# Three small instructions of the first five pairs move from VectorE to GpSimd, and the first block of x is loaded before the fifth pair's reciprocals

## The chip, the cores and the metric

The kernel runs on one core of a Trainium2 chip. The metric is the device time of one execution in microseconds (us); the time before is the median of three runs, 1360.91 us (1358.39 to 1362.42). The engines are named as in the profile: PE is TensorE (PEld its weight loads), DVE is VectorE, ACT is ScalarE, POOL is GpSimd, and SP is the engine from whose queue the DMAs are issued.

## The reference

Attention with a threshold, then a two-layer MLP with a parametric ReLU, all in float32:

```python
scores = scale * q @ k^T                       # 8 batches, 8 heads, 576 x 576, head_dim 64
scores = where(scores >= max - tau, scores, -1e9)
attn = exp(scores - max)
attn = attn / (sum(attn) + 1e-9)
x = (attn @ v), heads side by side             # 4608 tokens x 512
h = x @ w_in                                   # 512 -> 2048
out = (max(h, 0) + alpha * min(h, 0)) @ w_out  # 2048 -> 512
```

## The kernel before

Heads are worked in 32 pairs (four pairs of a batch). A pair has nine units of 128 query rows, and one unit is one cycle of the main loop `for i in range(-3, total + TAIL)`; unit u of pair p belongs to cycle 9p + u. A cycle does the mask of its own unit (DVE), the scores of the unit two cycles on (PE), row maxima (DVE) and exponentials (ACT), and the transposes of the masked exponentials (PE). Float32 products are made of high and low parts, so most operands are split in two, by ACT, DVE and POOL.

The other work is written out by hand in a table of cycles: `at_cycle(n, step)` puts a step into the list of cycle n, and when the loop comes to that cycle it issues the list in the order in which it was filled (all pairs first, then the decoding of weights). On PE, ACT, DVE and POOL the instructions run in exactly the order of issue. The order of SP's queue of DMAs is chosen at build time from when each DMA is taken to be ready, so it can differ from the order in the text.

The first five pairs (`WHOLE = 5`) are "whole": their products with v use unsplit operands. During cycles 0 to 48 the kernel also decodes the first 14 pieces of weights, each through a row of steps: five on ACT and DVE, then `rest` (four half-tile operations on POOL) and, one cycle later, `join` (two half-tile operations on POOL).

The division by the row sums is a tail of its own. With o = 9p, a whole pair's tail stands in the cycles o + `FINW`: `recip` (o+9) takes the nine column sums `sm` that the masks have accumulated, makes (sm + 1e-9) times min(sm + 1e-9, 1), and takes the reciprocal; `rturn` (o+10) transposes it on PE into a PSUM tile `rp`, one of four of the pool `ps_m`; `rout` (o+11) copies that out with ACT, stores it to DRAM (`rvd`) and loads it twice as a broadcast (`rb`); `fin_mul` (o+16) multiplies x by it on POOL; `fin_out` (o+17) stores x to DRAM (`xs`). Later pairs have their own table, `FINS`, and no minimum.

The MLP takes tokens in groups of 256. Cycle 49 makes the first two groups ready. `Mlp.step_l1` then loads the first group's x (`load_x`, cycle 49) and splits it into high and low parts on POOL (`split_part`, a copy and a subtraction for each of four chunks: two chunks in cycle 49 + `XO0`, two in the next), and from cycle 49 + `XO0` + 2 on one block of the first layer is issued in each cycle with room for it. A planner (`Mlp.cycle`) adds up the estimated PE time of each cycle for that; cycles with attention-times-v products of the split pairs take no such block. Cycles 4, 49 and 52 have three extra products (`filler`) on PE. After the last cycle `behind` does the rest of the MLP, which keeps PE busy alone.

Of the kernel before, what the change touches and what calls it, by code (L numbers as in the profile page):

```python
# [10 lines left out]
F32 = mybir.dt.float32  # L11
# [5 lines left out]
ALU = mybir.AluOpType  # L17
# [4 lines left out]
P = 128  # L22
# [24 lines left out]
AVW = (5, 7, 9, 11)  # L47
AVS = (5, 6, 10, 11)
FINW = (9, 10, 11, 14, 16, 17, 18)
FINS = (9, 11, 12, 12, 15, 16, 16)  # L50
ACTO, SPLO, PUTO = 1, 2, 1
TH1, TH2, TH3 = 0.75, -0.45, 0.1
XO, XO0 = 1, 2
L2O, L2O0 = 3, 1
P1 = 2
LD = 7
# [1 line left out]
WHOLE = 5  # L58
# [22 lines left out]
def tile_masked_attention_moe(  # L81
# [11 lines left out]
    nc = tc.nc  # L93
# [173 lines left out]
    ap1 = at.enter_context(tc.tile_pool(name="ap1", bufs=1))  # L267
# [35 lines left out]
    class Pair:  # L303
# [329 lines left out]

        def recip(self):
            self.rv = ap1.tile([P, 9], F32, tag="rv", name=f"rv{self.pi}", bufs=2)
            nc.vector.tensor_scalar(self.rv, self.sm, 1e-9, None, op0=ALU.add)
            if self.whole:
                nc.vector.scalar_tensor_tensor(self.rv, self.rv, 1.0, self.rv, op0=ALU.min, op1=ALU.mult)
            nc.vector.reciprocal(self.rv, self.rv)

        def rturn(self):
# [55 lines left out]
    def at_cycle(i, fn, *a):  # L697
        later.setdefault(i, []).append((fn, a))
# [5 lines left out]
    for p in pairs:  # L704
        o = 9 * p.pi
        n = o - 9
        if p.pi > 1:
            at_cycle(n + PREP["lk"], p.load, "k")
            at_cycle(n + PREP["lq"], p.load, "q")
        if p.pi == 1:  # L710
            n += P1
        if p.pi > 0:
            at_cycle(n + PREP["kh"], p.prep_kh)
            at_cycle(n + PREP["kl"], p.prep_kl)
            at_cycle(n + PREP["qh"], p.prep_qh)
            at_cycle(n + PREP["qs"], p.prep_qs)
            at_cycle(n + PREP["ql"], p.prep_ql)
            at_cycle(n + PREP["mk"], p.move_k)
            at_cycle(n + PREP["mk2"], p.move_k2)
            at_cycle(n + PREP["mq"], p.move_q)  # L720
            at_cycle(n + PREP["mq2"], p.move_q2)
            at_cycle(n + PREP["lv"], p.load, "v")
            at_cycle(n + PREP["vh"], p.prep_vh)
            at_cycle(n + PREP["vl"], p.prep_vl)
        fin = FINW if p.whole else FINS
        if p.whole:
            for c, step, j in zip(AVW, (0, 0, 1, 1), (0, 1, 1, 0)):
                at_cycle(o + c, p.avmul, step, j, range(3))
                at_cycle(o + c + 1, p.avmul, step, j, range(3, 5))
                at_cycle(o + c + 2, p.avout, step, j)  # L730
        else:
            for c, step, j in zip(AVS, (0, 0, 1, 1), (0, 1, 1, 0)):
                at_cycle(o + c, p.avmul, step, j)
                at_cycle(o + c + 1, p.avout, step, j)
        at_cycle(o + fin[0], p.recip)
        at_cycle(o + fin[1], p.rturn)
        at_cycle(o + fin[2], p.rout)
        at_cycle(o + fin[3], p.fin_add)
        at_cycle(o + fin[4], p.fin_mul)
        if not p.whole:  # L740
            at_cycle(o + fin[5], p.fin_un)
        at_cycle(o + fin[5 if p.whole else 6], p.fin_out)
# [398 lines left out]
    with tc.manual_schedule(engines=ENGINES) if ENGINES else ExitStack():  # L1141
        p = pairs[0]
# [116 lines left out]
```

## Time and profile before

| | before |
|---|---|
| median of three runs | 1360.91 us |
| the profiled execution's own time | 1360.37 us |
| its span, first to last instruction | 1358.6 us |
| mean granted TensorE clock | 0.999 |
| PE busy | 1324.9 us (98%) |
| DVE busy | 973.6 us (72%) |
| POOL busy | 970.8 us (71%) |
| ACT busy | 842.4 us (62%) |

The profile is of one execution. Shares are means over very different stages: the attention with weight decoding (to about 150 us), attention with the MLP beside it (to about 815 us), and the MLP alone. A timeline row gives the start, the busy time, the engine, the line of the kernel, the operation, out<-in and the number of instructions merged in it; in brackets stands how long the engine had been idle before it and what released it.

### The profile page before, as it was taken

How to read it: one execution, taken by the hardware profiler on the slowest of the kernel's cores; microseconds unless marked ns; L12 is line 12 of the kernel's file. 1: busy time of each engine (PE TensorE's matmuls, PEld its weight loads, DVE VectorE, ACT ScalarE, POOL GpSimd, SP SyncE). 2: the span in 40 equal slices, each digit the busy share in tenths (PEclk: the TensorE clock that was granted, in tenths of full speed). 3: DMA queues.
4: the chain of work that ended last, by engine and by line, in shares of the span. 5: the costliest groups of instructions: out<-in, count | busy, mean ns of one | idle time of the engine just before them, and what ended most of it. 6: DMA issues, size and time to landing. Idle time of an engine off the chain costs nothing.

```text
span 1358.6 us, 24051 instructions
## 1 busy us (share of the span) xinstructions
PE 1324.9 (98%) x8041; PEld 1162.3 (86%) x8041; DVE 973.6 (72%) x1843; ACT 842.4 (62%) x1910; POOL 970.8 (71%) x1369
## 2 busy tenths in 40 slices
PE   6988999999999999999999999999999999999999
PEld 4655799999999999999999999988888888888887
DVE  6989889889888888888888874665565744333332
ACT  7888888888888888888888873433332321211110
POOL 3766899899889898988988985775665754433431
PEclk9999999999999999999999999999999999999999
DMA  8653544644544645545445414345555443343222
GB/s 241 183 160 104 152 131 121 166 128 120 160 134 124 165 127 142 140 132 144 141 136 146 117 51 127 109 132 170 183 164 196 134 145 124 109 152 113 93 78 86
DMA packets 113595, 186.04 MB, mean 137 GB/s; under 512 B 16608, under 2 KB 47872, under 8 KB 113472
## 3 DMA queue, kind: packets, MB, share of 16 engines
q1 hardware_dynamic: 113152, 183.92, 46.2%
q8 instruction: 64, 1.05, 0.3%
q10 hardware_dynamic: 320, 0.59, 0.2%
q14 instruction: 59, 0.48, 0.1%
HBM read 104.41 MB, written 37.90 MB: 105 GB/s over the span
## 4 chain that ended last, share of the span: by engine, by line
PE 83%; DVE 6%; ACT 6%; POOL 1%; DMA 1%; issue 1%; ACTq 0%; SPq 0%; POOLq 0%; DVEq 0%
PE acca L256 12%; PE pha L226 12%; PE s L441 10%; PE phc L226 9%; PE av L620 8%; PE accc L256 8%; PE accb L256 7%; PE phb L226 7%; PE t L485 7%; DVE p L476 2%; DVE nmx L456 2%; PE tk L501 1%; PE accc L981 1%; ACT p L464 1%; ACT xh L205 1%
## 5 line engine op out<-in xcount | busy, mean ns | idle before, releaser
L456 DVE TENSOR_REDUCE nmx<-s 128x1 f32<-128x576 f32 x288 | 217.2, 754 | 67.8 <-PE s L441 65.3
L256 PE MATMUL acca<-wo,ga 128*128 128x512 f32 x756 | 224.1, 415 | 0.9 <-ACT xb L631 0.9
L476 DVE SCALAR_TENSOR_TENSOR p<-s,thr,p 128x576 f32<-128x576 f32 x256 | 206.6, 807 | 4.5 <-ACT thr L469 4.4
L464 ACT ACTIVATE p<-s,nmx 128x576 f32<-128x576 f32 x256 | 189.8, 741 | 8.7 <-DVE nmx L456 8.4
L441 PE MATMUL s<-kh,qst 128*128 128x288 f32 x640 | 141.6, 311 | 27.9 <-DVE p L476 16.2
L250 POOL TENSOR_TENSOR gc<-ptc,gc 128x512 fp32r<-128x512 f32 x45 | 58.1, 1292 | 144.0 <-ACT gc L247 144.0
L226 PE MATMUL pha<-xh,wi 128*128 128x256 f32 x784 | 157.9, 285 | 0.2 <-ACT pra L239 0.2
L485 PE MATMUL t<-ident,p 128*128 128x128 f32 x1024 | 154.5, 273 | 0.0
L247 ACT ACTIVATE gc<-ptc 128x512 fp32r<-128x512 f32 x45 | 28.4, 632 | 196.8 <-DVE ptc L951 196.8
L256 PEld LDWEIGHTS acca<-wo,ga 128*128 128x128 f32 x756 | 133.5, 190 | 19.1 <-ACT xb L631 1.4
L441 PEld LDWEIGHTS s<-kh,qst 128*128 128x128 f32 x640 | 100.1, 191 | 54.6 <-issue 26.4
L226 PEld LDWEIGHTS pha<-xh,wi 128*128 128x128 f32 x784 | 128.0, 190 | 6.5 <-ACT pra L239 3.6
L441 PE MATMUL s<-kl,qst 128*128 128x288 f32 x640 | 133.1, 298 | 0.0
L485 PEld LDWEIGHTS t<-ident,p 128*128 128x128 f32 x1024 | 124.4, 141 | 1.3 <-DVE e L551 1.0
L942 POOL TENSOR_TENSOR homexl<-homexr,homexh 128x512 fp32r<-128x512 f32 (+1 forms) x84 | 103.2, 1247 | 22.1 <-ACT homexh L941 22.0
L226 PE MATMUL phc<-homexh,wi 128*128 128x512 f32 x360 | 112.5, 389 | 0.0
L226 PE MATMUL pha<-xl,wi 128*128 128x256 f32 x392 | 110.7, 283 | 0.0
L578 POOL TENSOR_TENSOR rt<-kw,rt 64x128 fp32r<-64x128 f32 x216 | 97.8, 453 | 17.3
L256 PE MATMUL accc<-wo,gc 128*128 128x512 f32 x480 | 110.1, 389 | 0.0
L250 POOL TENSOR_TENSOR ga<-pta,ga 128x256 fp32r<-128x256 f32 x126 | 96.0, 763 | 18.5 <-ACT ga L247 10.1
L256 PEld LDWEIGHTS accc<-wo,gc 128*128 128x128 f32 x480 | 90.1, 188 | 18.7
L551 DVE TENSOR_TENSOR eo<-t,eo 128x512 fp32r<-128x512 f32 (+1 forms) x162 | 94.7, 598 | 12.7 <-ACT eo L547 11.5
(160 smaller groups left out, 3345.2 us busy)
## 6 DMA issues: line engine op xcount, KB each, us to landing
kr<-in_k_dram SPq DMA_DIRECT2D x31, 320.0 KB
rb<-rvd SPq DMA_DIRECT2D x64, 144.0 KB
xs<-xa SPq DMA_DIRECT2D x32, 288.0 KB
pinb<-part SPq DMA_DIRECT2D x36, 256.0 KB
part<-obb SPq DMA_DIRECT2D x36, 256.0 KB
pinc<-part SPq DMA_DIRECT2D x36, 256.0 KB
out_dram<-obc SPq DMA_DIRECT2D x35, 256.0 KB
qr<-in_q_dram SPq DMA_DIRECT2D x31, 288.0 KB
```

The lines of the kernel that those rows point to most:

```text
L226: nc.tensor.matmul(ph[:, :n], w[:, c, :], xx[:, c, :n], start=(c == 0 and ti == 0), stop=(c == NCC - 1 and ti == 2),)
L250: nc.gpsimd.tensor_tensor(g[:, 1, :n], t[:, :n], f(g[:, 0, :n]), op=ALU.subtract)
L256: nc.tensor.matmul(acc[:m, :], gg[:, g, o : o + m], w, start=(first and ti == 0), stop=(last and ti == 2))
L441: nc.tensor.matmul(ps[:, h, :288], w, kk[:, a + h * 288 : a + (h + 1) * 288], start=(ki == 0 and i == 0), stop=(ki == 1 and i == n - 1),)
L456: nc.vector.tensor_reduce(self.nmx[:, j : j + 1], self.S[u][0][:, :, :288], axis=AX.XY, op=ALU.max, negate=True)
L464: nc.scalar.activation(pj, ps[:, :, :288], AF.Exp, bias=nmx[:, j : j + 1], scale=1.0)
L476: nc.vector.scalar_tensor_tensor(pj, ps[:, :, :288], thr[:, j : j + 1], pj, op0=ALU.is_ge, op1=ALU.mult, accum_out=self.sm[:, c : c + 1])
L485: nc.tensor.transpose(tb[:, c, :], pt[:, j, j * D + c * P : j * D + (c + 1) * P], ident)
L551: nc.vector.tensor_tensor(dst[1], ps, f(dst[0]), op=ALU.subtract)
L578: nc.gpsimd.tensor_tensor(lo, r, f(hi), op=ALU.subtract)
L620: nc.tensor.matmul(pa[:m, :n], w, x, start=(part == 0 and c == 0), stop=c == NKC)
L942: self.low.tensor_tensor(xl[:, c, :n], xr[:, c, :n], f(xh[:, c, :n]), op=ALU.subtract)
```

## The change

For whole pairs, `recip` does the additions, the minimum and the product with three instructions on POOL, where it had two on DVE (an addition, and a minimum and product in one); the reciprocal itself stays on DVE. Split pairs are as before. The fifth pair (pair 4, the last whole one) gets a table of its own, `FINL`: `rturn` moves from cycle 46 to 48, `rout` from 47 to 50, `fin_mul` from 52 to 54 and `fin_out` from 53 to 55, so that `rout` comes after the cycle of the first `load_x`. `XO0` goes from 2 to 1: the first group's x is split in cycles 50 and 51 where it was 51 and 52, and the first layer may begin in cycle 52 where it was 53.

```diff
+FINL = (9, 12, 14, 14, 18, 19)
-XO, XO0 = 1, 2
+XO, XO0 = 1, 1
@@ recip
-            nc.vector.tensor_scalar(self.rv, self.sm, 1e-9, None, op0=ALU.add)
             if self.whole:
-                nc.vector.scalar_tensor_tensor(self.rv, self.rv, 1.0, self.rv, op0=ALU.min, op1=ALU.mult)
+                ru = ap1.tile([P, 9], F32, tag="ru", name=f"ru{self.pi}", bufs=1)
+                nc.gpsimd.tensor_scalar(ru, self.sm, 1e-9, 1.0, op0=ALU.add, op1=ALU.min)
+                nc.gpsimd.tensor_scalar(self.rv, self.sm, 1e-9, None, op0=ALU.add)
+                nc.gpsimd.tensor_tensor(self.rv, self.rv, ru, op=ALU.mult)
+            else:
+                nc.vector.tensor_scalar(self.rv, self.sm, 1e-9, None, op0=ALU.add)
             nc.vector.reciprocal(self.rv, self.rv)
...
-        fin = FINW if p.whole else FINS
+        fin = (FINW, FINL)[p.pi == WHOLE - 1] if p.whole else FINS
```

## Rows read from the trace of the kernel before

**Rows 1.** The page's chain that ended last, shares by engine, and busy time by engine in the stretch from 100 to 120 us (after the stretch: its length, then PE, PEld, DVE, ACT, POOL busy us with instruction counts, granted clock, DMA share, GB/s).

```profile
PE 83%; DVE 6%; ACT 6%; POOL 1%; DMA 1%; issue 1%; ACTq 0%; SPq 0%; POOLq 0%; DVEq 0%
...
100.00:120.00 20.00, 16.34 (x88) 10.79 (x89) 19.18 (x36) 16.88 (x37) 13.54 (x16) 1.00 0.51 143
```

**Rows 2.** Groups of DVE instructions by line, 0 to 160 us: busy us and mean ns of one.

```profile
L638 DVE SCALAR_TENSOR_TENSOR rv<-rv 128x9 f32<-128x9 f32 x5 | 3.2, 636 | 0.2
L636 DVE TENSOR_SCALAR rv<-sm 128x9 f32<-128x9 f32 x5 | 2.0, 406 | 0.0
L639 DVE RECIPROCAL rv<-rv 128x9 f32<-128x9 f32 x5 | 1.1, 216 | 0.2
```

**Rows 3.** Timeline of DVE and then of POOL around the first pair's reciprocals (cycle 9).

```profile
36.62 0.43 DVE L636 TENSOR_SCALAR rv<-sm 128x9 f32<-128x9 f32 x1
37.09 0.66 DVE L638 SCALAR_TENSOR_TENSOR rv<-rv 128x9 f32<-128x9 f32 x1
...
37.91 1.05 DVE L151 SCALAR_TENSOR_TENSOR wti<-wri,wti 128x512 int32<-128x512 int32 x1
...
36.30 1.42 POOL L77 TENSOR_TENSOR wti<-wti,wi 128x256 f32<-128x256 f32 x2
37.68 1.88 POOL L77 TENSOR_TENSOR wi<-wti,wri 128x256 fp32r<-128x256 f32 x2
```

**Rows 4.** The same for the second pair (cycle 18).

```profile
61.52 0.39 DVE L636 TENSOR_SCALAR rv<-sm 128x9 f32<-128x9 f32 x1
...
62.79 0.79 DVE L146 TENSOR_SCALAR wti<-wti 128x512 int32<-128x512 int32 x1
...
61.84 1.44 POOL L77 TENSOR_TENSOR wi<-wti,wri 128x256 fp32r<-128x256 f32 x2
```

**Rows 5.** The same for the third pair (cycle 27).

```profile
86.95 0.26 DVE L636 TENSOR_SCALAR rv<-sm 128x9 f32<-128x9 f32 x1
...
87.94 0.78 DVE L146 TENSOR_SCALAR wto<-wto 128x512 int32<-128x512 int32 x1
...
86.57 1.19 POOL L77 TENSOR_TENSOR wro<-wro 128x256 f32<-128x256 f32 x2
```

**Rows 6.** The same for the fourth pair (cycle 36), with one row of ACT.

```profile
112.02 0.53 DVE L636 TENSOR_SCALAR rv<-sm 128x9 f32<-128x9 f32 x1
...
113.41 0.81 DVE L156 TENSOR_SCALAR wro<-wto 128x512 int32<-128x512 int32 x1
...
112.47 1.43 POOL L77 TENSOR_TENSOR wo<-wto,wro 128x256 fp32r<-128x256 f32 x2
113.87 1.58 POOL L403 TENSOR_TENSOR qt<-qr,qst 128x576 fp32r<-128x576 f32 x1
...
113.94 0.63 ACT L160 ACTIVATE wo<-wto 128x512 fp32r<-128x512 f32 x1 [0.33 <-POOL wo L77]
```

**Rows 7.** The same for the fifth pair (cycle 45).

```profile
137.57 0.42 DVE L636 TENSOR_SCALAR rv<-sm 128x9 f32<-128x9 f32 x1
...
138.85 1.05 DVE L151 SCALAR_TENSOR_TENSOR wto<-wro,wto 128x512 int32<-128x512 int32 x1
...
138.62 1.87 POOL L77 TENSOR_TENSOR wo<-wto,wro 128x256 fp32r<-128x256 f32 x2
140.65 1.41 POOL L403 TENSOR_TENSOR qt<-qr,qst 128x576 fp32r<-128x576 f32 x1 [0.15 <-ACT qr L393]
```

**Rows 8.** POOL's smallest arithmetic, in a split pair's tail: timeline of three instructions of 64x1.

```profile
172.16 0.18 POOL L662 TENSOR_TENSOR xa<-xa,xb 64x1 f32<-64x1 f32 x1
172.43 0.21 POOL L663 TENSOR_SCALAR vs<-xa 64x1 f32<-64x1 f32 x1
172.70 0.19 POOL L662 TENSOR_TENSOR xa<-xa,xb 64x1 f32<-64x1 f32 x1
```

**Rows 9.** Timeline of PE: the scores that follow the first, fourth and fifth pair's reciprocals, with PE's idle time before them.

```profile
40.51 0.50 PE L441 MATMUL s<-kh,qst 128*128 128x288 f32 x2 [0.92 <-DVE p L476]
...
116.61 0.50 PE L441 MATMUL s<-kh,qst 128*128 128x288 f32 x2 [2.33 <-DVE p L476]
...
141.45 0.50 PE L441 MATMUL s<-kh,qst 128*128 128x288 f32 x2 [1.04 <-DVE p L476]
```

**Rows 10.** The one early stretch with a lower granted clock: a row of PE's timeline before it, and busy time and clock from 24 to 25 us (columns as in rows 1).

```profile
23.29 0.58 PE L441 MATMUL s<-kh,qst 128*128 128x288 f32 x2 [1.94 <-DVE p_t L476]
...
24.00:25.00 1.00, 1.00 (x7) 0.95 (x7) 1.00 (x3) 0.39 (x1) 0.83 (x2) 0.50 1.17 318
```

**Rows 11.** The first group's x, timeline: the issue of the fifth pair's broadcast and of x on SP's queue, POOL's first split, PE's scores after the filler of cycle 52, and (from the chain in order of time) a later block of the first layer alone.

```profile
146.89 1.10 SPq L652 DMA_DIRECT2D rb<-rvd  x2
148.04 0.59 SPq L200 DMA_DIRECT2D xr<-xs  x1
...
153.16 0.40 POOL L214 CAST xh<-xr 128x256 fp32r<-128x256 f32 x1 [0.42 <-DMA xr<-xs]
...
159.27 0.51 PE L441 MATMUL s<-kh,qst 128*128 128x288 f32 x2 [0.68 <-PE filler L691]
...
285.80 1.67 PE pha L226 x12
```

**Rows 12.** Timeline of ACT and PE in cycle 50, where the fifth pair's copy out of PSUM would come: ACT's last instruction before that place, and the cycle's transposes.

```profile
152.58 0.29 ACT L469 ACTIVATE thr<-nmx,ntau_sb 128x1 f32<-128x1 f32 x1
...
152.67 0.60 PE L485 MATMUL t<-ident,p 128*128 128x128 f32 x4
```

## The prediction

> **What bounds the kernel now.** I read the page's chain first: PE carries 83% of it, DVE 6%, POOL 1% [rows 1]. That is a mean over three stages, and the whole change lies in the first, so the stretch itself decides. From 100 to 120 us DVE is busy 19.18 of 20 us, PE only 16.34 and POOL 13.54 [rows 1]. The waits say the same: after three of the first five pairs' reciprocals PE stands idle for 0.92, 2.33 and 1.04 us until a DVE mask releases the scores [rows 9]. So up to about 150 us the pace is DVE's, and time given to or taken from DVE ahead of those masks reaches PE one for one. Later PE is the bound, in a fixed order, so a delay that PE takes in the first stage stays to the end. What is to be seen in the timelines of the five places [rows 3 to 7]: where DVE comes to `recip`, and what POOL still has in hand at that moment. POOL's mean load (13.54 of 20) does not show that.
>
> **Part 1: what leaves DVE.** Five additions of 406 ns and five min-and-products of 636 ns, in all 2.0 + 3.2 = 5.2 us on DVE [rows 2]. The reciprocal (216 ns) stays. For nine columns 406 and 636 ns are long, and the rows show why: in the first pair the min-and-product ends at 37.09 + 0.66 = 37.75, and POOL's two half-tiles beside it end at 36.30 + 1.42 = 37.72 [rows 3].
>
> The Trainium skill (SBUF — State Buffer, section "Who interferes with whom") says that a DVE instruction with two SBUF inputs, or in a 2-port mode, and a GpSimd instruction that reads SBUF exclude each other for the whole instruction; these ends agree with it. By that rule part of the 5.2 us is waiting that the next two-input or 2-port instruction on DVE inherits, so where POOL is reached early (the third pair, below) the gain would shrink by up to half a 1.19 us pair of half-tiles, and the sum below would be about 4.1 + 0.4 = 4.5 us in place of 4.1. No row here shows which of the two it will be.
>
> **Part 1: what comes onto POOL, and the new wait.** The reciprocal now waits for the third POOL instruction, and POOL takes its work strictly in order. `recip` stands ahead of the weight steps of the same cycle but behind everything of earlier cycles. POOL's smallest arithmetic runs 0.18 to 0.21 us and follows itself every 0.27 us (172.16, 172.43, 172.70) [rows 8]; so three take 0.27 + 0.27 + 0.21 = 0.75 us. The trace has none of 128x9. From below, three of 0.18 without a gap are 0.54; from above, three of the 0.40 us copy of 128x256 [rows 11] are 1.20. I take 0.75, the nearest row. Handing over costs 0.04: an ACT instruction that waits for a POOL `join` ending at 112.47 + 1.43 = 113.90 starts at 113.94 [rows 6]. From the end of the old min-and-product (37.75) to the first DVE instruction after the reciprocal (37.91) it is 0.16 [rows 3]. So DVE goes on 0.75 + 0.04 + 0.16 = 0.95 us after POOL reaches `recip`. Pair by pair, against the start of the same DVE instruction before:
>
> - First (cycle 9): POOL has the `rest` of cycle 8 in hand and starts the `join` behind `recip` at 37.68. 37.68 + 0.95 = 38.63 against 37.91: 0.72 later [rows 3].
> - Second (18): 61.84 + 0.95 = 62.79 against 62.79: nothing [rows 4].
> - Third (27): POOL is free for it at 86.57, before DVE comes (86.95). 87.52 against 87.94: 0.42 sooner [rows 5].
> - Fourth (36): the `join` of cycle 35 is ahead, and the next row starts at 113.87. 114.82 against 113.41: 1.41 later [rows 6].
> - Fifth (45): the `join` of cycle 44 is ahead; it began only at 138.62, after DVE had come at 137.57. It took 1.87 us beside DVE's work; the fourth pair's took 1.43 [rows 6, 7]. With DVE waiting it ends between 140.05 and 140.49, so DVE goes on at 141.00 to 141.44 against 138.85: 2.15 to 2.59, say 2.37 later [rows 7].
>
> Sum: 0.72 + 0 - 0.42 + 1.41 + 2.37 = 4.1 us lost. Behind the waiting reciprocal stand a decoding step, a row maximum and the mask for which PE is already idle, so nothing covers it: PE's gaps of 0.92, 2.33 and 1.04 us [rows 9] become about 1.6, 3.7 and 3.4. The three POOL instructions also push the queue behind them by 0.75 us; there stand a `join` and the low half of a later pair's q, needed several cycles later, so I take nothing.
>
> **Part 2: the fifth pair's tail, later.** `rturn` and `rout` are one PE and one ACT instruction, moved, not added; `rout`'s store and two loads go with it, `fin_mul` and `fin_out` follow two cycles later, and the fifth pair's x belongs to the second batch, not loaded before cycle 85: nothing. `rp` now holds its PSUM bank from cycle 48 to 50 instead of 46 to 47. Going through the tiles taken in cycles 49 and 50 I find one released in time for each, so nothing again; if the transposes of cycle 50 had to wait for the copy, which would run from 152.87 to about 153.15 against their start at 152.67, the cost would be 0.5 [rows 12]. Below nothing there is no way.
>
> **Part 2: x, sooner.** Before, x's load was issued at 148.04, directly behind the two broadcasts (146.89 + 1.10 = 147.99), and landed at 153.16, 5.1 us later, POOL having waited 0.42 for it [rows 11]. Without the store and broadcasts ahead it can go earlier, while the new stalls push POOL's place for the split back by some 4 us, less its one cycle of advance; so x is there. Then the first block comes in cycle 52. The planner's rule, followed cycle by cycle, gives first-layer blocks in cycles 52, 53, 54, 57, 58, 61, 62 where it was 53, 54, 57, 58, 61, 62, 63, and the second group starts in cycle 67 in both: the head start is used up there, since a new batch is only ready at cycle 85 anyway. What is left is that a block (at most 1.67 us) sits in cycle 52, where PE had 0.68 us idle [rows 11], and eleven second-layer products come earlier. If PE sets the pace throughout, that gains 0.68; if DVE sets it in the cycles that get lighter, it loses 1.67 - 0.68 = 1.0. I take 0, between the two.
>
> **The sum.** 4.1 + 0 = 4.1 us on the profiled execution's own 1360.37, that is 1364.5 (its span of 1358.6 would be 1362.7). That execution lies 0.54 us under the median of the runs, 1360.91; so against the median the forecast is 1365.0 us. 0.3% of it is 4.1 us, about the least that a measurement of this kernel tells from no change, so the forecast sits on that border.
>
> **The rivals.**
> - Forecast, 0.45: DVE stalls behind POOL's queue. Its own range, from the bounds of the small instructions (5 x -0.21 = -1.0; 5 x +0.45 = +2.2): 4.1 - 1.0 = 3.1 to 6.3 us, so 1364.0 to 1367.2.
> - The stall is there but smaller, 0.25: the instructions run at 0.54 together, the fifth pair's `join` at its quickest (2.15), and the idle slot of cycle 52 is filled: 4.1 - 1.0 - 0.2 - 0.7 = 2.2, so 1363.1. For it speaks that POOL has DVE's contention off it while DVE waits; against it that three of the five `join` or `rest` rows are already at their quick 1.42 to 1.44.
> - Faster, 0.10: POOL reaches `recip` first everywhere and the work removed is pure gain: 5.2 us, 1355.7. It decides from the point where POOL is free 0.95 us ahead of DVE's next instruction. For it speaks the third pair and POOL's low mean load; against it the fourth and fifth, where POOL's earlier work ends 1.9 and 2.9 us after DVE has come (113.90 against 112.02, 140.49 against 137.57).
> - The clock, 0.13: the longer gaps lower PE's granted clock. A gap of 1.94 us came before the one early fall to 0.50, the lower of the two levels, 1.2 GHz [rows 10]; but one of 2.33 at 116.61 brought none (1.00 over 100 to 120 us) [rows 1, 9]. Gaps of 3.7 and 3.4 us are longer than either. A fall of some 3 us at half clock, as from 24 to 27, costs about 1.5 each: 4.1 + 3.0, so 1368.0.
> - x does not go ahead, 0.07: SP's order is chosen at build time; if x still follows the broadcasts, POOL stands at the split for up to the 5.1 us of the load less its own lag, about 2 us, before work of pair 6: 1367.
>
> **How the numbers follow.** The time is the forecast's, 1365.0. From 1360.0 to 1369.0 the range holds the forecast, the smaller stall, the clock and x, and leaves out the faster case and a little at each end. Slower by over 0.3% (above 1365.0): half of the forecast with its longer upper side 0.25, the clock 0.12, x 0.06, the smaller stall 0.05, together 0.48. Faster by over 0.3% (below 1356.8): 0.09 of the 0.10. The rest, 0.43, is no change.
>
> **What would show it.** Right: in the new trace DVE idle ahead of the reciprocal by about 1 us in the first and second pair, 2.5 in the fourth, 3 to 3.5 in the fifth, nearly none in the third, released by a POOL product of 128x9; PE's gaps after the fourth and fifth pair above 3 us; x issued before the `rvd` store; a first-layer block in cycle 52, and the second group's blocks where they were. Wrong: reciprocals that start within 0.3 us of DVE's arrival, PE gaps no longer than before, or a place after cycle 63 where the head start is still there.

## The result, and the profile after

The changed kernel takes 1368.16 us (1367.33 to 1370.67), against 1360.54 us for the kernel before on the same chip (the three runs known ahead and one more): 7.6 us more, where 4.1 was forecast, a ratio of 1.006 (95% interval 1.0039 to 1.008). It is slower by more than measurement noise, inside the range, and 3.2 us above the forecast of 1365.0. The profiled execution's span is 1365.5 us where it was 1358.6, its mean granted clock 0.995 where it was 0.999.

DVE's instructions in the first 160 us, by line, where the two groups of small sums are gone and the reciprocal has a wait [rows 2]:

```profile
L644 DVE RECIPROCAL rv<-rv 128x9 f32<-128x9 f32 x5 | 1.1, 216 | 9.7 <-POOL rv L641 9.7
```

So 5.2 us of DVE work became 9.7 us of DVE waiting. The five waits, in the timeline of DVE (the bracket is the idle time before the instruction and what ended it), against [rows 3 to 7]:

```profile
38.23 0.21 DVE L644 RECIPROCAL rv<-rv 128x9 f32<-128x9 f32 x1 [2.00 <-POOL rv L641]
...
63.14 0.22 DVE L644 RECIPROCAL rv<-rv 128x9 f32<-128x9 f32 x1 [1.25 <-POOL rv L641]
...
87.90 0.22 DVE L644 RECIPROCAL rv<-rv 128x9 f32<-128x9 f32 x1 [0.55 <-POOL rv L641]
...
114.99 0.22 DVE L644 RECIPROCAL rv<-rv 128x9 f32<-128x9 f32 x1 [2.55 <-POOL rv L641]
...
143.46 0.21 DVE L644 RECIPROCAL rv<-rv 128x9 f32<-128x9 f32 x1 [3.38 <-POOL rv L641]
143.59 1.82 DVE L152 SCALAR_TENSOR_TENSOR wto<-wro,wto 128x512 int32<-128x512 int32 x1
```

The fifth, from POOL's side, answers to [rows 7]: the join, then the three new instructions, then the low half of q. From the start of the first small instruction to the start of the next piece of work it is 143.47 - 142.57 = 0.90 us.

```profile
141.05 1.43 POOL L78 TENSOR_TENSOR wo<-wto,wro 128x256 fp32r<-128x256 f32 x2
142.57 0.27 POOL L639 TENSOR_SCALAR ru<-sm 128x9 f32<-128x9 f32 x1
142.89 0.24 POOL L640 TENSOR_SCALAR rv<-sm 128x9 f32<-128x9 f32 x1
143.22 0.21 POOL L641 TENSOR_TENSOR rv<-rv,ru 128x9 f32<-128x9 f32 x1
143.47 1.40 POOL L404 TENSOR_TENSOR qt<-qr,qst 128x576 fp32r<-128x576 f32 x1
```

PE's gaps after the first, fourth and fifth pair, 0.92, 2.33 and 1.04 us in [rows 9], are now:

```profile
40.98 0.50 PE L442 MATMUL s<-kh,qst 128*128 128x288 f32 x2 [1.85 <-DVE p L477]
...
117.81 0.50 PE L442 MATMUL s<-kh,qst 128*128 128x288 f32 x2 [3.12 <-DVE p L477]
...
146.97 0.82 PE L442 MATMUL s<-kh,qst 128*128 128x288 f32 x2 [4.10 <-DVE p L477]
```

And with the last two the clock goes down, which it did not there before. In the busy time by stretches (columns as in [rows 1]) the granted clock is the figure before the DMA share: 0.50 of full speed, the lower of the two levels (1.2 GHz). After the fourth pair it falls just behind the gap; at the fifth it is down already before the gap ends at 146.97, with PE busy for 0.04 us from 146 to 147 us.

```profile
119.00:120.00 1.00, 1.00 (x5) 0.55 (x4) 1.00 (x2) 0.58 (x4) 1.00 (x2) 0.50 0.85 336
120.00:121.00 1.00, 1.00 (x4) 0.46 (x2) 1.00 (x3) 1.00 (x3) 0.91 (x2) 0.50 0.35 139
...
146.00:147.00 1.00, 0.04 (x1) 0.07 (x1) 1.00 (x4) 0.88 (x3) 0.00 (x0) 0.50 0.72 154
...
149.00:150.00 1.00, 1.00 (x4) 0.52 (x3) 0.16 (x1) 0.64 (x2) 0.28 (x1) 0.50 0.00 0
150.00:151.00 1.00, 1.00 (x3) 0.23 (x1) 0.69 (x1) 0.94 (x3) 0.82 (x3) 0.50 0.00 0
```

Where the time goes is best read by cycles. The table gives the lag of each run against the kernel before: the start of the cycle's transposes (PE) in that run's timeline minus the start in the timeline of before. The other columns are the experiments below, in their order; each is one profiled execution. Cycle 9 lies ahead of the first reciprocal: what a column shows there (-0.57 to +0.77) is a difference between executions, so each column is read from its own value at cycle 9.

```
cycle            changed  x only  sums   gaps    recip.  ACT     join
                                  only   filled  later   later   later
 9               -0.47    -0.57   +0.77  +0.21   -0.04   +0.14   +0.76
11 (pair 1 past) +0.29    -0.37   +0.71  +0.97   +0.14   -0.60   +2.95
18               +0.28    -0.38   +0.70  +0.97   +0.14   -0.39   +2.95
20 (pair 2 past) +0.29    -0.38   +0.69  +0.96   -0.27   -0.81   +3.90
27               +0.31    -0.41   +0.68  +0.96   -0.26   -0.80   +3.89
36 (pair 3 past) +0.41    -0.63   +0.60  +0.86   -0.78   -1.10   +3.99
37               +1.20    -0.77   +1.58  +1.79   -3.14   -3.46   +3.25
38 (pair 4 past) +2.45    -0.77   +2.79  +1.84   -1.93   -3.43   +3.34
45               +2.45    -0.77   +2.80  +1.85   -1.92   -2.05   +3.34
46               +6.00    -0.79   +6.28  +4.79   -3.00   -3.14   +4.25
47 (pair 5 past) +8.06    -0.80   +8.65  +4.79   -1.69   -2.97   +4.25
60               +7.85    -0.99   +8.66  +4.56   -1.91   -3.21   +4.80
82               +8.10    -0.76   +8.64  +4.82   -1.65   -2.95   +4.27
```

In the changed kernel the lag comes in five steps, and all of it is there by cycle 47: cycles 9 to 11 (the first pair's wait, +0.76), 36 to 37 (the fourth wait, +0.8), 37 to 38 (+1.25, under the low clock), 45 to 46 (the fifth wait, +3.55, the end of it under the low clock), 46 to 47 (+2.06, under the low clock). From 47 on it stands within 0.3 us at the cycles shown. Later, between cycles 133 and 143, it shrinks by 1.2 us and is 6.9 us in the last cycle. The kernel with x alone shrinks as much there (-0.51 to -1.73), so this does not come from the reciprocals' waits; its cause is open.

### The profile page after: what moved, and what is told of

The parts are those of the page before. It is cut to its first block, busy times and chain, and to the rows that moved or that the text cites. A ratio compares the mean times of both kernels' runs of the same rounds, so it can differ in the third digit from the quotient of the medians.

```text
span 1365.5 us, 24042 instructions
## 1 busy us (share of the span) xinstructions
PE 1327.4 (97%) x8041; PEld 1164.2 (85%) x8041; DVE 970.7 (71%) x1833; ACT 842.1 (62%) x1910; POOL 973.9 (71%) x1384
## 3 DMA queue, kind: packets, MB, share of 16 engines
q8 instruction: 64, 1.05, 0.3%
## 4 chain that ended last, share of the span: by engine, by line
PE 85%; ACT 5%; DVE 4%; POOL 3%; issue 2%; DMA 1%; ACTq 0%; SPq 0%; POOLq 0%; DVEq 0%
PE acca L257 12%; PE pha L227 12%; PE s L442 10%; PE phc L227 9%; PE av L621 9%; PE accc L257 8%; PE t L486 7%; PE accb L257 7%; PE phb L227 7%; DVE p L477 1%; PE tk L502 1%; DVE nmx L457 1%; PE accc L986 1%; ACT p L465 1%; ACT xh L206 1%
```

## The experiments

Theory: DVE's reciprocal waits out POOL's queue; PE's gaps grow by that, and the two longest lower the clock; moving x is worth nothing. Rivals: the moved x costs part of it; the steps in cycles 38 and 47 are DVE held by POOL and not the clock; the wait is a fixed price of going to POOL and back.

**The part with x alone.** The changed kernel with `recip` as it was:

```diff
+            nc.vector.tensor_scalar(self.rv, self.sm, 1e-9, None, op0=ALU.add)
             if self.whole:
-                ru = ap1.tile([P, 9], F32, tag="ru", name=f"ru{self.pi}", bufs=1)
-                nc.gpsimd.tensor_scalar(ru, self.sm, 1e-9, 1.0, op0=ALU.add, op1=ALU.min)
-                nc.gpsimd.tensor_scalar(self.rv, self.sm, 1e-9, None, op0=ALU.add)
-                nc.gpsimd.tensor_tensor(self.rv, self.rv, ru, op=ALU.mult)
-            else:
-                nc.vector.tensor_scalar(self.rv, self.sm, 1e-9, None, op0=ALU.add)
+                nc.vector.scalar_tensor_tensor(self.rv, self.rv, 1.0, self.rv, op0=ALU.min, op1=ALU.mult)
```

> The changed kernel with the small sums back on DVE as before; the fifth pair's later tail and the earlier x stay. Theory (all of the loss comes from the reciprocals' wait for POOL and what follows from it): 1360.5 us, within 1 us of before; the lag against the kernel before is 0 at cycle 45, and at most +0.5 us after cycle 70. Rival (moving x and the fifth pair's tail costs by itself, since the lag grew by 1 us between cycles 61 and 65): 1361.5 to 1362.5 us. Second rival (the head start of a block is worth something): 1359 to 1360 us.

Measured: 1359.56 us against 1360.27 for before in this set, ratio 0.9996 (0.9987 to 1.0004): no change that the runs resolve. The rival that moving x costs is out; the 0.7 us under before would also fit the second rival, which the interval neither shows nor excludes. The lag is the same in cycles 45 and 82 (-0.77 and -0.76): the head start is used up, as forecast. That x really went ahead of the reciprocals here is in SP's queue:

```profile
143.10 0.59 SPq L201 DMA_DIRECT2D xr<-xs  x1
148.03 0.33 SPq L334 DMA_DIRECT2D kr<-in_k_dram  x1
152.24 0.29 SPq L649 DMA_DIRECT2D rvd<-rt  x1
```

In SP's queue of the changed kernel x also goes ahead of that store (which comes at 161.10), but behind the next load of k:

```profile
155.39 0.33 SPq L334 DMA_DIRECT2D kr<-in_k_dram  x1
155.78 0.43 SPq L201 DMA_DIRECT2D xr<-xs  x1
```

and in POOL's timeline of the same kernel the split stood 1.38 us for it, where it had been 0.42 [rows 11]. That cost PE nothing that stayed: the lag is 8.06 in cycle 47 and 8.10 in cycle 82.

```profile
159.97 0.40 POOL L215 CAST xh<-xr 128x256 fp32r<-128x256 f32 x1 [1.38 <-DMA xr<-xs]
```

**The small sums alone.** The kernel before with only the new `recip`:

```diff
-            nc.vector.tensor_scalar(self.rv, self.sm, 1e-9, None, op0=ALU.add)
             if self.whole:
-                nc.vector.scalar_tensor_tensor(self.rv, self.rv, 1.0, self.rv, op0=ALU.min, op1=ALU.mult)
+                ru = ap1.tile([P, 9], F32, tag="ru", name=f"ru{self.pi}", bufs=1)
+                nc.gpsimd.tensor_scalar(ru, self.sm, 1e-9, 1.0, op0=ALU.add, op1=ALU.min)
+                nc.gpsimd.tensor_scalar(self.rv, self.sm, 1e-9, None, op0=ALU.add)
+                nc.gpsimd.tensor_tensor(self.rv, self.rv, ru, op=ALU.mult)
...
```

> The kernel before with only the whole pairs' small sums on POOL. Theory: the whole loss comes back, 1367.5 to 1368.5 us, with DVE idle 2.0, 1.25, 0.55, 2.5 and 3.4 us before the five reciprocals, and the granted clock lowered twice, after the fourth and the fifth. Rival (the two parts only lose together): under 1365 us.

Measured: 1367.78 us, ratio 1.005 (1.0038 to 1.0063). The whole loss is in this part. The waits before the reciprocals are 1.42, 1.23, 0.56, 2.74 and 3.38 us; the first is smaller than expected by 0.6. In that execution PE had stood 0.75 us for a DMA of q at 32.29, so DVE came later to this place and had less to wait; the lag shows it (+0.77 already at cycle 9, and no step at the first pair). The low clock comes again with the fourth and fifth.

The single executions say something of their own here. Five of the six have a mean granted clock of 0.995 or 0.996 and take 1367.12 to 1368.69 us; one has 0.999, as the kernel before has in most, and takes 1362.82. So the one execution that by its mean clock had no such falls is some 5 us faster than the other five.

**Work for PE in the gaps.** Filler products behind the attention-times-v products of the fourth and fifth pair; nothing else changes:

```diff
+    for i, n in ((36, 9), (45, 12)):
+        at_cycle(i, filler.run, n)
```

> The changed kernel with 9 more filler products behind the attention-times-v products of cycle 36 and 12 behind those of cycle 45, so that PE works through most of the two long gaps; DVE and POOL do what they did. Theory (the lag that comes one cycle after each gap, 1.25 us in cycle 37 and 2.06 us in cycle 46, is the lowered clock): the granted clock stays at 1.00 there and the time falls by 3.3 us to about 1364.9 us, while DVE's waits before the reciprocals stay as they are. Rival (those steps are DVE held by POOL, not the clock): 1367.5 to 1368.5 us, or slower by what fillers run past the end of the gap.

Measured: 1364.56 us, ratio 1.0035 (1.0022 to 1.0048). The theory had 1364.9. PE's timeline at the fourth pair, with the filler and what is left of the gap:

```profile
115.08 2.27 PE L696 MATMUL filler<-ident 128*128 128x128 f32 x18
118.37 0.53 PE L442 MATMUL s<-kh,qst 128*128 128x288 f32 x2 [1.01 <-DVE p L477]
```

The busy time of the same run in the two stretches that had the low clock; the clock is now 1.00 in both:

```profile
117.00:123.00 6.00, 4.86 (x31) 3.55 (x30) 6.00 (x13) 3.93 (x10) 4.25 (x6) 1.00 0.45 137
146.00:153.00 7.00, 6.79 (x39) 4.89 (x40) 6.14 (x15) 4.38 (x11) 4.79 (x10) 1.00 0.49 145
```

DVE waits just as long (2.73 and 3.39 us), and more useless work is done, yet the time is 3.2 us under the sums alone on the same chip (1367.78; that kernel lacks the moved x, worth 0.7 us by the medians above, if anything). The two intervals overlap, but of the executions only that one at clock 0.999 lies under these five (1364.29 to 1366.55). The steps in cycles 38 and 47 are gone (1.79 to 1.84, 4.79 to 4.79). They were the clock.

**The reciprocal one cycle later.** The POOL instructions stay where they are; the reciprocal, and with it the tail of the first four pairs, comes a cycle on, so that DVE meets it when POOL is done:

```diff
-FINW = (9, 10, 11, 14, 16, 17, 18)
+FINW = (9, 11, 12, 14, 16, 17, 18)
-            nc.vector.reciprocal(self.rv, self.rv)
+            if not self.whole:
+                self.recip2()
...
+        def recip2(self):
+            nc.vector.reciprocal(self.rv, self.rv)
...
+        if p.whole:
+            at_cycle(o + fin[0] + 1, p.recip2)
```

> The changed kernel with the whole pairs' reciprocal issued one cycle after the three POOL instructions, and the transpose and the copy out of the first four pairs a cycle later as well. Theory (the loss is only the place of the wait): no DVE wait over 0.3 us before the five reciprocals, no gap of PE above 2.5 us, full clock, and faster than before by up to the 5.2 us of the two removed DVE instructions: 1355.5 to 1359 us, the nearer to 1359 the more of the 5.2 us was waiting for POOL that the next DVE instruction inherits. Rival (POOL's longer queue costs by itself): 1361 us or more.

Measured: 1359.10 us, ratio 0.9991 (0.9982 to 1.0). The loss is gone: the largest wait for POOL is 0.17 us, the clock 1.00 around all five. The time lies just outside the expected 1355.5 to 1359 us: of the 5.2 us taken from DVE only 1.2 us arrive against before, and 0.5 us against x alone (1359.56), neither clear of noise. The lag falls in three places (-0.04 to -1.00 in cycle 10, -0.78 to -3.14 in 37, -1.92 to -3.00 in 46), and about 1.2 us of it comes back each time in the next cycle. At the first and the fifth DVE now waits for ACT:

```profile
42.16 0.82 DVE L477 SCALAR_TENSOR_TENSOR p<-s,thr,p 128x576 f32<-128x576 f32 x1 [1.14 <-ACT thr L470]
...
139.20 0.69 DVE L552 TENSOR_TENSOR e<-t,e 128x512 fp32r<-128x512 f32 x1 [1.06 <-ACT e L548]
```

At the fourth the trace has no wait for ACT: there the decoding step behind the reciprocal took 1.48 us (from 114.29, beside a POOL instruction of 1.41 us from 114.08), where the same step took 0.69 before. Over the stretch from 20 to 155 us ACT is the larger part. The largest of DVE's waits for ACT, first with x alone and then here (total us, times, longest):

```profile
DVE p L477 <- ACT thr L470: 4.4, 7, 1.0
...
DVE p L477 <- ACT thr L470: 6.6, 9, 1.1
```

All of DVE's waits for ACT together are 6.6 us with x alone and 9.9 us here. So 3.3 of the 5.2 us went into waits for ACT and 0.6 into longer decoding (38.9 to 39.5 us); the 1.3 us left fit the 1.4 us by which this column falls further than that of x alone between cycles 9 and 82. This is the account of one execution of each.

**One ACT instruction later.** In those five cycles ACT prepares q for the pair after next, two instructions of 0.68 us. One moves a cycle on, on top of the last kernel:

```diff
-            at_cycle(n + PREP["qs"], p.prep_qs)
+            at_cycle(n + PREP["qs"] + (2 <= p.pi <= WHOLE + 1), p.prep_qs)
```

> The kernel with the reciprocal one cycle later (the run before), and one of the two ACT instructions that prepare q for the pair after next (0.68 us, in the reciprocals' cycles) moved one cycle on, for these five pairs only. Theory (the 5.2 us taken from DVE came to only 1.2 us because ACT is late next: DVE then waited 1.1 us for ACT in cycles 10 and 46): another 0.3 to 0.6 us a pair, so 1356 to 1358 us. Rival (what was gained is held up by POOL through the shared port, or by PE): 1358.5 to 1360 us, as the run before.

Measured: 1358.70 us, ratio 0.9991 (0.9983 to 1.0) against 1359.76 for before in this set; a miss of the expected 1356 to 1358, and no clear gain over the last kernel (1.1 us under before, against 1.2). Its profile does move the way that was expected (lag -2.97 in cycle 47 where it was -1.69; DVE's total wait for `thr` 4.9 us where it was 6.6), but one execution's lag is not its median: DVE's gains of a microsecond are at the edge of what these runs resolve. It is not shown to be faster than before, its interval reaches 1.0. So that ACT holds up what DVE saved is read from the traces, and this experiment, which should have shown it in the time, did not.

**The joins one cycle later.** The changed kernel, with the last POOL step of every weight piece a cycle on:

```diff
-        at_cycle(c + 6, lambda w=w, fc=fc, io=io: (w.join(...
+        at_cycle(c + 7, lambda w=w, fc=fc, io=io: (w.join(...
```

> The changed kernel with the last step of each weight piece (the join, two half-tiles on POOL, 1.43 us) one cycle later, so that in the fourth and fifth pair it stands behind the small sums and not ahead of them; it is the same work. Theory (DVE's wait is the length of POOL's queue at that place): DVE's waits before the fourth and fifth reciprocal fall by about 1.4 us each, from 2.5 and 3.4 to 1.1 and 2.0 us, those of the first three stay within 0.4 us; PE's two long gaps fall to about 1.8 and 2.8 us. The time falls by 2.9 us to 1365.3 us if the clock still drops twice, to 1362 us if neither gap lowers it, in between if one does. Rival (the wait is a fixed cost of going over to POOL and back, not the queue): 1367 to 1369 us.

Measured: 1365.32 us, ratio 1.0042 (1.003 to 1.0054). The five waits:

```profile
40.84 0.22 DVE L644 RECIPROCAL rv<-rv 128x9 f32<-128x9 f32 x1 [3.39 <-POOL rv L641]
67.19 0.22 DVE L644 RECIPROCAL rv<-rv 128x9 f32<-128x9 f32 x1 [2.63 <-POOL rv L641]
91.48 0.21 DVE L644 RECIPROCAL rv<-rv 128x9 f32<-128x9 f32 x1 [0.56 <-POOL rv L641]
117.16 0.21 DVE L644 RECIPROCAL rv<-rv 128x9 f32<-128x9 f32 x1 [1.13 <-POOL rv L641]
142.95 0.21 DVE L644 RECIPROCAL rv<-rv 128x9 f32<-128x9 f32 x1 [1.97 <-POOL rv L641]
```

The fourth and fifth fall by one join each, 1.42 and 1.41 us, as expected. The first and second rise by 1.39 and 1.38, which was not: there the shift brought an earlier piece's join behind the low half of k, which starts late because it waits for ACT, and so into the queue ahead of the sums. POOL's timeline of this run at the first pair has that join between the low half of k and the `rest`, and the sums behind:

```profile
34.07 1.69 POOL L78 TENSOR_TENSOR kl<-kr,kh 128x320 fp32r<-128x320 f32 x2 [6.26 <-ACT kh L369]
35.72 1.61 POOL L78 TENSOR_TENSOR wi<-wti,wri 128x256 fp32r<-128x256 f32 x2
...
39.92 0.28 POOL L639 TENSOR_SCALAR ru<-sm 128x9 f32<-128x9 f32 x1
```

The sum of the five waits is 9.7 us in both kernels. That settles the mechanism in both directions: the wait is the length of POOL's queue at that place, join by join, and not a fixed price. The time is 5.6 us over before (1359.76 in this set), where the changed kernel's is 7.6 over: 2.1 us less, with intervals that overlap. In the profiled execution no gap lowered the clock: it is 1.00 behind the fourth and the fifth, and also behind the first, now PE's longest, as its timeline and the busy time of the stretch behind it show:

```profile
43.65 0.50 PE L442 MATMUL s<-kh,qst 128*128 128x288 f32 x2 [3.29 <-DVE p L477]
```

```profile
42.00:48.00 6.00, 4.35 (x28) 3.37 (x29) 5.51 (x12) 3.96 (x9) 5.63 (x8) 1.00 0.63 186
```

That is not so in every execution of it: three have a mean clock of 0.996 or 0.997 and take 1365.95 to 1367.78 us, three have 0.998 or 0.999 and take 1363.47 to 1364.69. These three lie 3.7 to 4.9 us over before, about the 4.3 us of the kernel with the gaps filled, whose five waits add up to nearly the same (9.9 us). So the median agrees with the expected 1365.3 by luck: that figure supposed 2.8 us less of waiting and two falls of the clock, and what came is as much waiting as ever and fewer falls.

## Why the prediction was right, and where it was not

**What bounds the stage: right.** The loss is in the first 150 us and reaches PE one for one: in the run with the gaps filled DVE's balance is 9.9 us of waiting less 5.2 us of work, 4.7 us, and PE's lag 4.6. It stays, but for the 1.2 us that come back between cycles 133 and 143.

**The waits: right in kind, and nearly in size.** The place in POOL's queue was as read. That the first wait would be about 1 us, as named among the signs of being right, does not follow from the prediction's own rows: DVE at 36.62 and POOL done at 37.68 + 0.79 = 38.47 make 1.85, and 2.00 was measured. Of the sizes, "three take 0.75 us" was a little low: the rows after show 0.86 from the start of the first to the end of the third (142.57 to 143.43), since 128x9 runs 0.27, 0.24 and 0.21 us and not 0.18 to 0.21, and follows after 0.32 and 0.33 us and not 0.27. Without the clock, in the run with the gaps filled, the waits cost the steps of the table: first pair 0.76 (forecast 0.72), second 0 (0), third with the cycles up to 36 -0.10 (-0.42), fourth 0.98 (1.41), fifth 2.94 (2.37): 4.6 us together against the forecast 4.1, and 4.3 us by that run's median over before (1364.56 against 1360.27). That the sum comes so near is in part luck: the fourth was forecast too large, and the third and the fifth too small.

The fifth was too small because the next DVE instruction, a decoding step with two inputs in SBUF, took 1.82 us and not 1.05 (1.75 with the gaps filled): it began at 143.59, just after POOL's 1.40 us instruction (143.47 to 144.87), and ran to 145.41. That is the exclusion which the prediction cited from the Trainium skill (SBUF — State Buffer, "Who interferes with whom"), and here it fits; the prediction had looked for it at the third pair only. At the fourth it went the other way: before, the two decoding steps behind the reciprocal took 0.81 and 1.60 us (from 113.41), in the changed kernel 1.47 and 0.41 (from 115.12), and DVE made good 0.5 us of the wait. Over all the decoding steps from 20 to 155 us it is small: DVE's eight groups add up to 38.9 us before, 39.6 in the changed kernel and 39.5 with the reciprocal later, so not more than 0.7 of the 5.2 us was inherited in this way.

**"The clock", 0.13: this rival came true.** It was priced at 3.0 us on top and a time of 1368.0; measured are 3.3 us (7.6 over before, against 4.3 with the gaps filled) and 1368.16, and all four executions of the changed kernel have a mean clock of 0.995 or 0.996. The step that failed is the likelihood: the prediction foresaw gaps of 3.7 and 3.4 us (they are 3.12 and 4.10), had a gap of 2.33 that did nothing and none longer to go by, and left the fall at about one in eight. That is why the measured time lies 3.2 us above the forecast, and why the chance for slower (0.48) looks too low; the range held because it had been drawn to take in this rival.

**x: right that it is worth nothing** (0, with bounds of -0.7 and +1.0; measured -0.7 us with an interval that includes none). The planner's blocks came as forecast: the traces of the changed kernel and of x alone have first-layer blocks in cycles 52, 53, 54, 57, 58, 61 and 62, and the second group from cycle 67. x went ahead of the `rvd` store in both, so the rival in which it follows the broadcasts did not come true. In the changed kernel it stood behind a load of k instead, which the prediction did not have (with the gaps filled, also both parts, it stood ahead of that load, at 145.76); the wait that followed was 1.38 us on POOL and nothing lasting on PE.

**"Faster", 5.2 us: wrong as a price also.** Even with POOL out of the way only 1.2 us of it arrives, 0.5 of it over x alone. The traces put most of the rest to waits for ACT, which no time has confirmed. The prediction counted what DVE loses, and did not ask which engine has the next instruction ready last.

## What to carry to other kernels

An instruction handed from a busy engine to one that is idle a third of the time gains only if its place in the second engine's queue is reached in time: look up what that engine still has in hand at that very moment, not its share of busy time, or let the result be taken up a step later. Price a stall on the engine that feeds PE twice, once as the stall and once as what the granted clock may do after the gap. And before crediting time taken off the pacing engine, look in the trace for the engine that would be late next.

## What was not expected of the hardware

Which gap lowers the granted clock is not told by its length alone. Gaps of 3.12 and 4.10 us (changed kernel) and 3.31 and 4.02 us (the sums alone) came with a fall to 0.50; one of 3.29 us (joins later, first pair) and one of 2.33 us [rows 9] were followed by 1.00, while one of 1.94 us came before the early fall [rows 10]. That early fall is in five of the eight profiled executions, each time behind a gap of 1.93 to 1.96 us; in the other three (x alone, the reciprocal later, ACT later) PE has no gap above 1.1 us at that place, from 20 to 25 us, and keeps 1.00. Nor does one program always do the same: an execution of the sums alone kept a mean clock of 0.999 where five fell to 0.995 or 0.996. The runs don't settle what else counts, and the document leaves it open.

A PE gap of about 1.3 us at the end of cycle 61, ahead of scores whose releaser the profile does not show, is in the kernel with x alone and in the changed one and not in the one before. It is also with the gaps filled, the reciprocal later and ACT later, but not with the joins later. The lag takes it back by cycle 82; its cause is open.
